# Zero fills of two gradient caches: nine fills on fifteen DMA engines become fills on sixteen, and four fills change place

## The chip, the core and the metric

The kernel runs on one core of a Trainium2 chip. A core has TensorE (matmuls, called PE in the profile), VectorE (DVE), ScalarE (ACT), GpSimd (POOL) and SyncE (SP), and sixteen DMA engines that carry all transfers between its on-chip memory and HBM. Transfers are issued by an engine's instruction stream, here mostly GpSimd's and SyncE's. The metric is the device time of one execution in microseconds (us), the median of several runs.

## What is computed

The reference is one decode step of a small transformer block with adaptive layer norm, its attention over a sliding window of a cache, a gated feed-forward part (FFN), and the gradients of all of it:

```python
mod = silu(c) @ w_mod                      # sa, ca, ga, sb, cb, gb
h = layernorm(x) * (1 + ca) + sa
x = x + ga * attention(h, k_cache, v_cache, wq, wo)   # the last 4096 of 65536 positions
h = layernorm(x) * (1 + cb) + sb
x = x + gb * ((sigmoid(h @ w_gate) * (h @ w_up)) @ w_down)
out, vjp = jax.vjp(f, x, k_cache, v_cache, wq, wo, w_gate, w_up, w_down, c, w_mod)
```

The outputs are `out` and a gradient for each input. What matters here are the gradients of the two caches (`out_2`, `out_3`): each is 4 heads x 65536 positions x 128 numbers in bf16, 64 MiB. Attention reads only the last 4096 positions, so the gradient of the first 61440 is zero. These zeros have to be written: 120 MiB, about half of all bytes that the kernel moves.

## The kernel before

**The zero fills.** The region of zeros of each head is seen as 128 rows of 61440 numbers and cut into 15 pieces of 128 rows x 4096 numbers, 1 MiB each; 2 caches x 4 heads x 15 pieces give 120 fills. A fill is one DMA from the small tile `zeros` on chip, issued by GpSimd. The list `zleft` holds them in order, and `zero(n, after)` (L147 to L171) issues the next `n`, if wanted not before a given instruction.

Of the 120 fills, 111 are wide (L169): 128 rows over all sixteen DMA engines, eight rows each. Nine are narrow (their places in the list are in `NARROW`). A narrow fill is two transfers. A piece of five rows of 512 bytes, in two halves (L162), takes the engines 0 to 4 after the cursor that deals out engines has been reset. It is followed by 120 of the 128 rows (L165), which take the next fifteen engines, so that the engine with index `SKIP` = 4 is left out. The eight rows left out of each narrow fill are written elsewhere: in the nine small pieces, and once near the start in `zero_rest` (two transfers, L361 and L364, of 540 KB and 13.5 KB).

**Where they are issued.** There is no scheduler: the order of instructions on each engine is the order of the program text. Counts written by hand say how many fills are issued at each point: `Z_Q` in the query projection, `Z_N` in the stage that forms a large product of keys and weighted values (`n_ps`, L636), `Z_B` in the chunks of the product with the output weights (`b_ps`, L691; called B), `Z_FOLD` at the end of the stage that folds the modulation weights, `Z_FFN` in the seven blocks of the FFN (four counts for each), `Z_END` in the last stage. GpSimd also issues most loads and stores in the same stream, so a fill stands in line with them.

**An FFN block.** The FFN's 3584 columns go through in seven blocks of 512. For block `q` the kernel forms the gradients of `w_up` and `w_gate` in place and stores them in two halves (`store_ug`, L868), with `zero(z[0])` and `zero(z[1])` behind these. It then starts block `q+1` with `front`, and handles its rows of `w_down` in two halves `s`: the forward matmul (`ffn_mm`, L970), a reduction (`wd_ttr`, L210), the gradient in place (`wd_outer`, L206) and its store (`store_wd`, L854). `zero(z[2])` follows the first half, `zero(z[3])` the second. The loads of block `q+2` are `load_ug` (L864, GpSimd) and `load_wd` (L851, SyncE); `load_wd` overwrites the buffer of the rows just stored, so it waits until that store has landed.

**The last stage** forms the remaining gradients (`wo`, `w_mod`, the window of the caches, `wq`) and stores them as they are ready; the kernel ends with stores of 512 KB to 1 MB, issued by GpSimd (L1125, L1130, L1166, L1173, L1177).

Of the kernel before, what the change touches and what calls it, by code (L numbers as in the profile page):

```python
# [10 lines left out]
P = 128  # L11
FP32 = mybir.dt.float32
# [21 lines left out]
EPS = 1e-5  # L34
SCALE = DH ** -0.5
KIB = 512
SKIP = 4
NARROW = (6, 18, 31, 44, 57, 70, 83, 96, 108)

def spread(total, n):
    return [(i + 1) * total // n - i * total // n for i in range(n)]
# [8 lines left out]
Z_KC = [0] * 8  # L51
Z_SM = 4
Z_N = spread(31, 128)
Z_B = [n + (i in (31, 38)) for i, n in enumerate(spread(29, 43))] + [1, 1, 1, 1, 0] + [1, 1, 0, 1, 1, 0, 1, 1] + [1, 0, 1, 0, 1, 0, 0, 0]
Z_FOLD = (1, 1, 3)
Z_FFN = [(1, 1, 0, 1)] * 5 + [(1, 1, 1, 2), (1, 2, 1, 0)]
Z_END = (1, 2, 1, 0, 0)
@with_exitstack
def kernel(
# [26 lines left out]
    nc = tc.nc  # L86
    SKW = A_k_cache.shape[2] - W
# [16 lines left out]
    def vt(shape, name, dt=FP32):  # L104
        return pool.tile(shape, dt, name=name)
# [4 lines left out]
    ZW = 4096  # L110
    zeros = vt([P, ZW // 2], "zeros", FP8)
# [11 lines left out]
    zregions = []  # L123
    for og in (out_2, out_3):
        for g in range(G):
            region = og[0, g, 0:SKW, :].rearrange("r d -> (r d)").rearrange("(p x) -> p x", p=P)
# [1 line left out]
                zregions.append(region[:, i * ZW:(i + 1) * ZW])  # L128

    narrow = zregions[0:len(NARROW)]
    wide = zregions[len(NARROW):]
    zleft = []
    while narrow or wide:
        if narrow and (len(zleft) in NARROW or not wide):
            zleft.append((narrow.pop(0), True))
        else:
            zleft.append((wide.pop(0), False))
    nlen = len(NARROW)
    ncount = list(range(1, nlen + 1))  # L140
    NS = SKIP + 1
    rest = out_2[0, 0, 0:SKW, :].rearrange("r d -> (r d)").rearrange("(p x) -> p x", p=P)[0:8, 0:nlen * ZW].bitcast(FP32)
    assert nlen * 2 <= 20

    keep = [0]

    def dep(later, earlier):  # L147
        tc.add_manual_dep(later.ins, earlier.ins.name,
                          mybir.DependencyInfo(mybir.DependencyClass.Sync, mybir.DependencyReason.DATA),
                          reason="pace")  # L150

    def zero(n, after=None):
        for _ in range(n):
            if len(zleft) <= keep[0]:
                return
            region, narrow_ = zleft.pop(0)
            first = None
            if narrow_:
                nc.gpsimd.inc_swdge_sem([], [], mode="reset_dge_cursor")  # L160
                n = nlen - ncount.pop()
                first = nc.gpsimd.dma_start(  # L162
                    out=rest[0:NS, 0:nlen * 128].rearrange("p (t x) -> p t x", t=2)[:, :, n * 64:(n + 1) * 64],
                    in_=zeros[0:NS, 0:64].rearrange("p (t x) -> p t x", t=1).broadcast_to([NS, 2, 64]))
                ins = nc.gpsimd.dma_start(  # L165
                    out=region[8:P, :].bitcast(FP32).rearrange("(t p) x -> p t x", t=2),
                    in_=zeros[0:60, :].rearrange("p (t x) -> p t x", t=1).broadcast_to([60, 2, ZW // 2]))
            else:
                ins = nc.gpsimd.dma_start(out=region.bitcast(FP32), in_=zeros[:, :])  # L169
            if after is not None:  # L170
                dep(first or ins, after)  # L171

    rot = [(psum, "mm")]
# [13 lines left out]
    def new_tp(name="tp"):  # L188
        p, tag = next_pool()
        return p.tile([P, 1024], BF16, name=name, tag=tag)  # L190
# [165 lines left out]
        nc.sync.dma_start(out=wq_t[j], in_=wq_view[:, j, :])  # L356
    load_kv(A_v_cache, v_nat)

    def zero_rest(after):
        wr = nlen * 120  # L360
        ins = nc.gpsimd.dma_start(out=rest[:, nlen * 128:].rearrange("p (t x) -> t p x", t=16),  # L361
                                  in_=zeros[0:16, 0:wr].rearrange("t (p x) -> t p x", p=1).broadcast_to([16, 8, wr]))
        dep(ins, after)
        nc.gpsimd.dma_start(out=rest[NS:8, 0:nlen * 128], in_=zeros[0:8 - NS, 0:nlen * 128])  # L364

    tp0 = new_tp("tp_rows")[:, 0:24]
    nc.tensor.transpose(tp0, rows24[:, :], ident_bf[0:24, 0:24])
    vecs = vt([P, 24], "vecs")
# [36 lines left out]
    for j in range(KD):  # L405
        for k in range(16):
            mm = nc.tensor.matmul(mod_ps[:, k:k + 1], lhsT=wm01_t[j][:, k * P:(k + 1) * P],
                                  rhs=cs_bf[:, j:j + 1], start=(j == 0 and k == 0), stop=(j == KD - 1),
                                  skip_group_check=True)
# [28 lines left out]
    jobs = []  # L438
# [24 lines left out]
    for j in range(KD):  # L463
        if j in (1, 2, 3):
            kT_unit(8 + 2 * j)
            kT_unit(9 + 2 * j)
        if 0 < j <= NT:
            for g in range(G):
                wqT_unit(j - 1, g, "AVAA"[g])
        for h in range(HQ):  # L470
            mm = nc.tensor.matmul(q_ps[:, h:h + 1], lhsT=wq_t[j][:, h * P:(h + 1) * P],  # L471
                                  rhs=h1_bf[:, j:j + 1], start=(j == 0 and h == 0), stop=(j == KD - 1),
                                  skip_group_check=True)
        zero(Z_Q[j], mm)
    zero_rest(mm)
    nc.scalar.activation(out=warm, in_=ones_f[:, 0:1], func=ACT.Exp)
    q_col2 = vt([P, 2 * HQ], "q_col2", BF16)
    cp(q_col2[:, 0:HQ], q_ps[:, 0:HQ])
# [4 lines left out]
    for ch in range(8):  # L483
        ps = new_ps("sc_ps")
        for g in range(G):
            mm = nc.tensor.matmul(ps[32 * g:32 * g + 32, 0:512], lhsT=q_col2[:, HG * g:HG * g + 32],
                                  rhs=k_T[:, g, ch * 512:(ch + 1) * 512], start=True, stop=True,
                                  tile_position=(0, 32 * g))
        nc.scalar.copy(out=P_bf[:, ch * 512:(ch + 1) * 512], in_=ps[:, :])
        nc.vector.reduce_max(out=mx8[:, ch:ch + 1], in_=ps[:, :], axis=AX.X)  # L490
        if ch % 2:
            wqT_unit(KD - 1, ch // 2, "AV"[ch // 2 % 2])
        zero(Z_KC[ch], mm)
# [115 lines left out]
    def mod_gb(ts_):  # L609
        ps = new_acc("g_ps")  # L610
        mod_tiles(ps, g_t, ts_, True, ts_[-1])
        if ts_[0] == 6:
            cp(gb, ps[:, 0:KD])
        else:
            addv(gb, gb, ps[:, 0:KD])
# [5 lines left out]
    def recent(mm, lag):  # L621
        last_mm.append(mm)
        return last_mm[-lag] if len(last_mm) >= lag else last_mm[0]

    for g in range(G):
        nbank = bank_pair("n_ps", g)
        for t_ in range(KT):
# [7 lines left out]
            for k in range(2):  # L635
                mm = nc.tensor.matmul(nbank[k][:, :], lhsT=k_nat[:, g, t_ * DH:(t_ + 1) * DH],  # L636
                                      rhs=vp[:, t_ % 2, 4 * k:4 * k + 4, :].rearrange("p h d -> p (h d)"),
                                      start=(t_ == 0), stop=False)
# [25 lines left out]
    bq = []  # L664
# [16 lines left out]
    def bch(n=1):  # L681
        for _ in range(n):
# [5 lines left out]
            for a in range(4):  # L688
                h = 4 * u + a
                for k in range(2):  # L690
                    mm = nc.tensor.matmul(bbank[p][k][:, :], lhsT=a4[:, p, h, :], rhs=wo_t[u][:, a, k * 512:(k + 1) * 512],  # L691
                                          start=(i == 0 and a == 0), stop=(i == 7 and a == 3))
            zero(Z_B[nbq - 1 - len(bq)], recent(mm, 3))
            if i == 7:
# [87 lines left out]
    def park(p, pl, tag):  # L782
        BT_ps[p] = pl.tile([P, D], BF16, name="BT_ps", tag=tag)
        for i in range(KD):
            nc.tensor.transpose(BT_ps[p][:, i * P:(i + 1) * P], B_t[p][:, i * P:(i + 1) * P], ident_bf[:, :])
# [64 lines left out]
    def load_wd(q, s):  # L850
        nc.sync.dma_start(out=wd_v[:, 2 * s:2 * s + 2, :], in_=wd_dram(B_w_down, q, s))  # L851
# [10 lines left out]
    def load_ug(q, j0, n):  # L862
        for k, view in ((0, wu_view), (1, wg_view)):
            nc.gpsimd.dma_start(out=ug_tile(q, k, j0, n), in_=ug_part(view, q, j0, n))  # L864
# [5 lines left out]
    def fold_half(t, k):  # L870
        ps = new_ps("fold_ps")
        for i in range(4):
            nb = 4 * k + i
            for x, src in enumerate((ga_t[t], cb_t[t], sb_t[t])):
                nc.tensor.matmul(ps[:, i * P:(i + 1) * P], lhsT=src[:, nb * P:(nb + 1) * P], rhs=ident_bf[:, :],  # L875
                                 start=(i == 0 and x == 0), stop=(x == 2), skip_group_check=True)
        nc.scalar.copy(out=w2_t[t][:, k * 512:(k + 1) * 512], in_=ps[:, :])  # L877
# [45 lines left out]
    fold_half(7, 1)  # L923
    zero(Z_FOLD[0])
    park(4, ppq, "pq")
    load_ug(1, 0, 4)
    load_ug(1, 4, 4)
    zero(Z_FOLD[1])
    mod_gb((0, 1, 2, 3, 4, 5))
# [48 lines left out]
    def wd_outer(q, s):  # L978
        for i in (2 * s, 2 * s + 1):
            outer_dve(wd_v[:, i, :], small[q % 2]["hh"][:, i:i + 1], b1k)  # L980
        store_wd(q, s)
# [30 lines left out]
    wd_outer(0, 1)  # L1012
    zero(Z_FOLD[2])
    load_wd(1, 0)
    load_wd(1, 1)
    for q in range(NB):
        z = Z_FFN[q]
        more = q + 1 < NB
# [282 lines left out]
    s2(7)  # L1301
    keep[0] = 0
    zero(len(zleft))
    assert not zleft and not narrow and not jobs and not bq

# [1 line left out]
_INS = ['A_x', 'A_k_cache', 'A_v_cache', 'A_wq', 'A_wo', 'B_x', 'B_w_gate', 'B_w_up', 'B_w_down', 'c', 'w_mod', 'grad_out']  # L1307
# [26 lines left out]
```

## Time and profile before

The time is 600.43 us (median of 3 runs, 600.42 to 600.61). The profiled execution has a span of 600.9 us.

| What | Value |
|---|---|
| bytes moved by DMA | 246.64 MB, mean 410 GB/s |
| read from HBM, written to HBM | 60.30 MB, 185.60 MB |
| transfers in GpSimd's queue (q0) | 216.55 MB |
| transfers in SyncE's and ScalarE's queue (q1) | 29.37 MB |
| wide fills, 1024 KB each | 111, 14.6 us from issue to landing (median) |
| narrow fills, 960 KB each | 9, 14.1 us |
| small pieces of the narrow fills, 2.5 KB each | 9, 12.4 us |
| `zero_rest`, 540 KB and 13.5 KB | 10.8 us and 10.5 us |
| a fill's instruction on GpSimd | 0.53 us wide, 0.60 and 0.67 us for the two of a narrow one |

A page of the profile gives for each engine its busy time and share, then the span in 40 slices of 15 us with a digit for the busy tenths of each, the DMA row and the rate of the transfers. The views of waits name the engine and line that waited, after "<-" what ended the wait, then total us, how many times, and the longest. The chain of waits is followed back from the last instruction; each piece of it is listed with its start, its length and what it was spent on.

### The profile page before, as it was taken

The numbers are of one execution on the slowest core, as the hardware profiler recorded it, in microseconds if no ns is written. First come the engines' busy times: TensorE is split into PE (matmuls) and PEld (weight loads), VectorE is DVE, ScalarE is ACT, GpSimd is POOL, SyncE is SP. The second block draws the span as 40 slices with busy tenths as digits, with TensorE's granted clock in tenths as the row PEclk, the third lists the DMA queues.
The fourth block names the chain that finished last, engine by engine and source line by source line (L and its number), as shares of the span: only waits on it lengthen the run. The fifth ranks groups of instructions, "written<-read, shape, count | busy, mean of one in ns | idle before, by whom it ended". The sixth has DMA issues, their size and how long they took to land.

```text
span 600.9 us, 11073 instructions
## 1 busy us (share of the span) xinstructions
PE 411.7 (69%) x4612; PEld 276.5 (46%) x4612; DVE 327.1 (54%) x620; ACT 284.7 (47%) x429; POOL 164.2 (27%) x265
## 2 busy tenths in 40 slices
PE   3997689999999989999985245444444196856300
PEld 3995334334344546546554234434434175655300
DVE  3654499999511010160008286695686888768430
ACT  3489514567212014212226556965857866863200
POOL 0003123223222222222322324333343253222230
PEclk9999699999999999999985555555555586755555
DMA  8999999999999999999999999999999999999995
GB/s 349 420 417 422 413 424 412 427 423 424 426 423 425 423 427 422 423 424 425 420 404 406 418 374 401 398 409 415 406 413 415 418 406 414 419 425 427 422 417 240
DMA packets 45171, 246.64 MB, mean 410 GB/s; under 512 B 5253, under 2 KB 5253, under 8 KB 24712
## 3 DMA queue, kind: packets, MB, share of 16 engines
q0 software_dynamic: 38976, 216.55, 94.4%
q1 hardware_dynamic: 6096, 29.37, 12.6%
q8 instruction: 36, 0.59, 0.4%
q14 instruction: 15, 0.12, 0.1%
q10 hardware_dynamic: 48, 0.01, 0.0%
HBM read 60.30 MB, written 185.60 MB: 409 GB/s over the span
## 4 chain that ended last, share of the span: by engine, by line
PE 40%; DMA 28%; DVE 17%; ACT 8%; issue 4%; POOL 0%; ACTq 0%; POOLq 0%; SPq 0%; DVEq 0%
DMA out_dram<-arena 19%; PE b_ps L691 17%; PE n_ps L636 6%; DMA arena<-in_B_w_down_dram 6%; DVE junk L210 4%; DVE arena L193 4%; DVE arena L206 4%; ACT arena L241 3%; DMA arena<-in_B_w_gate_dram 3%; PE t_ps L598 2%; DVE arena L210 2%; PE w_ps L394 2%; PE tp_wq L453 2%; PE fold_ps L875 1%; PE tp_k L434 1%
## 5 line engine op out<-in xcount | busy, mean ns | idle before, releaser
L691 PE MATMUL b_ps<-arena 128*128 128x512 bf16 x512 | 116.2, 379 | 0.0
L169 POOL DMA_DIRECT2D out_dram<-zeros x111 | 60.4, 545 | 197.3 <-PE q_ps L471 50.9
L836 PE MATMUL tp_side<-ident_bf,arena 128*128 128x128 bf16 x432 | 52.5, 303 | 45.9 <-ACT arena L837 39.0
L837 ACT COPY arena<-tp_side 128x1024 bf16<-128x1024 bf16 x54 | 53.9, 1012 | 52.5 <-PE tp_side L836 52.0
L193 DVE TENSOR_TENSOR arena<-arena 128x2048 bf16<-128x2048 bf16 x64 | 76.5, 1223 | 2.3 <-PE n_ps L636 0.3
L691 PEld LDWEIGHTS <-arena 128*128 128x128 bf16 x512 | 48.8, 98 | 55.8 <-issue 2.9
L210 DVE CUSTOM_DVE_ANT_0 arena<-arena,scr 128x1024 bf16<-128x1024 bf16 x56 | 65.2, 1220 | 10.3 <-ACT scr L990 10.3
L636 PE MATMUL n_ps<-arena 128*128 128x512 bf16 x256 | 65.7, 378 | 6.2 <-DVE arena L193 4.6
L836 PEld LDWEIGHTS <-arena 128*128 128x128 bf16 x432 | 43.6, 140 | 50.4 <-issue 50.1
L241 ACT ACTIVATE arena<-scr,h 128x1024 bf16<-128x1024 bf16 x56 | 61.5, 1146 | 1.4 <-DVE dh2acc L210 1.3
L636 PEld LDWEIGHTS <-arena 128*128 128x128 bf16 x256 | 24.6, 97 | 41.6 <-issue 16.2
L210 DVE CUSTOM_DVE_ANT_0 junk<-arena,b1k 128x1024 bf16<-128x1024 bf16 x28 | 34.2, 1222 | 11.6 <-DMA arena<-in_B_w_down_dram 11.1
L1161 ACT ACTIVATE arena<-ps_kv 128x512 bf16<-128x512 f32 x48 | 26.2, 686 | 28.8 <-PE ps_kv L1157 28.5
L868 POOL DMA_DIRECT2D out_dram<-arena x28 | 21.0, 755 | 64.8 <-ACT arena L241 40.3
L202 DVE CAST arena<-b_ps 128x512 bf16<-128x512 f32 x6 | 4.1, 691 | 61.6 <-PE b_ps L691 61.6
L600 ACT CAST arena<-t_ps 128x512 bf16<-128x512 f32 x56 | 30.1, 589 | 12.1 <-PE t_ps L598 12.1
L1157 PE MATMUL ps_kv<-junk,arena 8*128 8x128 bf16 x256 | 27.3, 305 | 11.7 <-DVE arena L206 10.6
L1157 PEld LDWEIGHTS <-arena 8*128 8x128 bf16 x256 | 25.3, 141 | 13.5 <-issue 13.5
L455 ACT COPY arena<-tp_wq 128x1024 bf16<-128x1024 bf16 x23 | 21.7, 1044 | 8.2 <-PE tp_wq L453 8.2
L970 PE MATMUL fg<-hh_bf,arena 128*128 128x1 bf16 x224 | 8.2, 166 | 22.7 <-DMA arena<-in_B_w_down_dram 20.9
L877 ACT CAST arena<-fold_ps 128x512 bf16<-128x512 f32 x16 | 9.4, 586 | 24.1 <-PE fold_ps L875 24.1
L206 DVE TENSOR_SCALAR arena<-arena,cs_col 128x4096 bf16<-128x4096 bf16 (+1 forms) x16 | 16.0, 1018 | 8.3 <-DMA out_dram<-arena 8.2
(299 smaller groups left out, 644.4 us busy)
## 6 DMA issues: line engine op xcount, KB each, us to landing
out_dram<-zeros POOLq DMA_DIRECT2D x111, 1024.0 KB, 14.6
out_dram<-arena POOLq DMA_DIRECT2D x32, 1024.0 KB, 18.2
out_dram<-arena POOLq DMA_DIRECT2D x50, 512.0 KB, 9.6
out_dram<-zeros POOLq DMA_DIRECT2D x9, 960.0 KB, 14.1
arena<-in_A_wq_dram SPq DMA_DIRECT2D x8, 1024.0 KB, 20.5
arena<-in_A_wo_dram POOLq DMA_DIRECT2D x8, 1024.0 KB, 12.2
arena<-in_w_mod_dram POOLq DMA_DIRECT2D x7, 1024.0 KB, 18.6
arena<-in_B_w_down_dram SPq DMA_DIRECT2D x14, 512.0 KB, 8.2
```

The costliest lines, as they stand in the source:

```text
L169: ins = nc.gpsimd.dma_start(out=region.bitcast(FP32), in_=zeros[:, :])
L193: return nc.vector.tensor_tensor(out=out, in0=a, in1=b, op=op)
L206: return nc.vector.tensor_scalar(out=out, in0=a, scalar1=s1, scalar2=None, op0=op0)
L210: return nc.vector.tensor_tensor_reduce(out=out, in0=w, in1=b, scale=1.0, scalar=0.0, op0=ALU.mult, op1=ALU.add, accum_out=acc)
L241: return nc.scalar.activation(out=out, in_=b, func=ACT.Copy, scale=col)
L600: nc.scalar.copy(out=o, in_=ps)
L636: mm = nc.tensor.matmul(nbank[k][:, :], lhsT=k_nat[:, g, t_ * DH:(t_ + 1) * DH], rhs=vp[:, t_ % 2, 4 * k:4 * k + 4, :].rearrange("p h d -> ...
L691: mm = nc.tensor.matmul(bbank[p][k][:, :], lhsT=a4[:, p, h, :], rhs=wo_t[u][:, a, k * 512:(k + 1) * 512], start=(i == 0 and a == 0), stop= ...
L836: nc.tensor.transpose(tp[:, i * P:(i + 1) * P], blk[:, i * P:(i + 1) * P], ident_bf[:, :])
L837: nc.scalar.copy(out=blk if dst is None else dst, in_=tp[:, :])
L1157: nc.tensor.matmul(ps[:, t4 * DH:(t4 + 1) * DH], lhsT=rows[32 * g:32 * g + HG, t_ * P:(t_ + 1) * P], rhs=hd[32 * g:32 * g + HG, :], start= ...
L1161: nc.scalar.activation(out=o, in_=ps[:, :], func=ACT.Copy, scale=float(scale))
```

## The change

All 120 fills become wide: nothing is skipped, `zero_rest` and the small pieces are gone, and the list of fills is simply the list of regions. With it four fills change place. One chunk of B loses its fill (`Z_B`), the two at the end of the fold stage go (`Z_FOLD`), and the last FFN block loses one (`z[2]` of the last entry). They return in the FFN: one more in the blocks 0, 1 and 2 between the two halves of `w_down`, and one more in block 5. The change makes all fills alike and spreads them more evenly over the FFN.

```diff
-SKIP = 4
-NARROW = (6, 18, 31, 44, 57, 70, 83, 96, 108)
...
-Z_B = [n + (i in (31, 38)) for i, n in enumerate(spread(29, 43))] + [1, 1, 1, 1, 0] + [1, 1, 0, 1, 1, 0, 1, 1] + [1, 0, 1, 0, 1, 0, 0, 0]
-Z_FOLD = (1, 1, 3)
-Z_FFN = [(1, 1, 0, 1)] * 5 + [(1, 1, 1, 2), (1, 2, 1, 0)]
+Z_B = [n + (i in (31, 38)) for i, n in enumerate(spread(29, 43))] + [1, 1, 1, 1, 0] + [1, 1, 0, 1, 1, 0, 1, 1] + [1, 0, 0, 0, 1, 0, 0, 0]
+Z_FOLD = (0, 0, 3)
+Z_FFN = [(1, 1, 1, 1)] * 3 + [(1, 1, 0, 1)] * 2 + [(1, 1, 1, 3), (1, 2, 0, 0)]
...
-            region, narrow_ = zleft.pop(0)
-            first = None
-            if narrow_:
-                nc.gpsimd.inc_swdge_sem([], [], mode="reset_dge_cursor")
-                n = nlen - ncount.pop()
-                first = nc.gpsimd.dma_start(
-                    out=rest[0:NS, 0:nlen * 128].rearrange("p (t x) -> p t x", t=2)[:, :, n * 64:(n + 1) * 64],
-                    in_=zeros[0:NS, 0:64].rearrange("p (t x) -> p t x", t=1).broadcast_to([NS, 2, 64]))
-                ins = nc.gpsimd.dma_start(
-                    out=region[8:P, :].bitcast(FP32).rearrange("(t p) x -> p t x", t=2),
-                    in_=zeros[0:60, :].rearrange("p (t x) -> p t x", t=1).broadcast_to([60, 2, ZW // 2]))
-            else:
-                ins = nc.gpsimd.dma_start(out=region.bitcast(FP32), in_=zeros[:, :])
+            ins = nc.gpsimd.dma_start(out=zleft.pop(0).bitcast(FP32), in_=zeros[:, :])
...
-    zero_rest(mm)
```

## The prediction

> **What bounds the kernel.** I start with the slices and the share of each engine.
>
> ```profile
> PE 411.7 (69%) x4612; PEld 276.5 (46%) x4612; DVE 327.1 (54%) x620; ACT 284.7 (47%) x429; POOL 164.2 (27%) x265
> ...
> DMA  8999999999999999999999999999999999999995
> GB/s 349 420 417 422 413 424 412 427 423 424 426 423 425 423 427 422 423 424 425 420 404 406 418 374 401 398 409 415 406 413 415 418 406 414 419 425 427 422 417 240
> ```
>
> No compute engine is over 69% of the span, while the DMA row shows 9 from the second slice to the last but one. The rate is 412 to 427 GB/s up to slice 19 and 374 to 418 in slices 21 to 34, mostly the FFN blocks. The program is a transfer program: 246.64 MB, of which 120 MiB are the zero fills. A change in fills matters through the sixteen DMA engines, not through an instruction.
>
> Next, who waits for transfers: GpSimd's waits over the whole span, TensorE's in the FFN (310 to 486 us), and SyncE's.
>
> ```profile
> POOL out_dram L169 <- DMA out_dram<-zeros: 43.3, 24, 3.2
> ...
> PE fg L970 <- DMA arena<-in_B_w_down_dram: 20.9, 10, 7.8
> ...
> SPq L851 <- DMA out_dram<-arena: 140.1, 12, 30.5
> ```
>
> GpSimd waits 24 times for an earlier fill to land. The reason is in the completion semaphores: its transfers take eight of them in turn, so a fill is issued only when the transfer eight before it has landed on all sixteen engines. Example: the fill issued at 259.24 follows the landing, at 258.71, of the one issued at 240.18. So the last of the sixteen engines sets the pace of issue. The w_down lines close a loop in the FFN: a load waits for the store of the same buffer, and TensorE and VectorE wait for the load.
>
> Last, the chain of waits from 484 us:
>
> ```profile
> 508.42 21.89 DMA out_dram<-arena
> ...
> 545.95 19.75 DMA out_dram<-arena
> ...
> 568.74 14.47 DMA out_dram<-arena
> ```
>
> The end is a full store queue. What the last engine still has to move then is end time, one for one.
>
> **Reading single DMA engines.** The trace holds sixteen completion times for each transfer, without engine numbers. I sort the sixteen of each GpSimd transfer and compare each with the ninth ("the middle"). A 1 MiB fill lands 2.44 us after the one before it (middle of 110), so an engine's 64 KB share costs 2.44 us.
>
> Narrow fills stand out. At the one issued at 138.10 (L165) one engine goes from 1.56 ahead of the middle (L162's piece, 148.38) to 3.92 ahead (the next wide fill, 153.15). That engine is the one skipped. The other eight show the same step: **2.33 us each**.
>
> Between narrow fills this engine falls back, smoothly: 3.92 to 3.06 ahead (153 to 185 us), 5.35 to 4.18 (190 to 222), 6.57 to 5.64 (227 to 257), 8.70 to 7.23 (268 to 297). The others keep their places but for single jumps. It loses 0.86 us in 32, 1.17 in 32, 0.93 in 30, 1.47 in 29: about 3% to 5%, taken as **3.1%**. So the skipped engine is a slow one. In the busy stage it is still over-relieved: 7 us ahead at 297 us, 8.9 ahead of the second earliest at 305.
>
> **What the Trainium skill says.** "DMA: Bandwidth & Descriptors", section "Why a DMA increments its semaphore by 16 and not by 1": on GpSimd's path all sixteen engines post a completion whatever the shape, and a transfer over fewer engines takes consecutive ones from a cursor. The trace agrees: even a five-row piece has sixteen completions, and one engine lands about 0.2 us after its last work while the others need 2.25. Same page, "Latency and other measured facts": engines 7 and 15 are usually slower in traces. The trace has no engine numbers and the kernel skips index 4, so only "one is slower" is confirmed, at 3.1%. Same page, "Anatomy of one DMA": about 2.0 us fixed plus bytes over 436e3. For 512 KB that is an estimate of 3.2 us; the store issued into a nearly empty queue at 480.86 took 3.37 to the middle landing. A latency above that is queue.
>
> **The change, part by part.**
>
> 1. Pieces that disappear. L361 costs 64.97 - 63.58 = 1.39 us of every engine, L364 0.19, nine L162 0.2 each = 1.8. Sum **3.4 us less** for all engines. Bytes are the same: 111 + 9 whole fills.
>
> 2. GpSimd's instructions. Eleven fewer, at 0.53 to 0.60 us (lines L361, L364, L162), and nine of 0.67 become 0.53: 7.6 us. GpSimd is 27% busy and waits for landings; hidden behind those waits, priced at nothing.
>
> 3. The slow engine's share. It now takes part in nine more fills: 9 x 2.33 = **21.0 us more** work.
>
> 4. The credit it wasted before. An engine far ahead runs dry, since GpSimd holds back for the last engine. From 305 to 356 us the skipped engine goes from 8.9 us ahead of the second earliest to level; 1.7 of these are its own slowness, some 1.7 more fall to reordering with SyncE's loads, leaving 5.5. Smaller losses of the same kind: 1.4 at 92 us, 0.7 at 376, 1.0 at 475 to 484, 0.8 in scattered places. Sum **9.4 us** idle before that work can fill.
>
> 5. Idle time shared by all. The middle engine shows some 3 us of gaps from 300 to 490 us (1.05 at 357, others of 0.1 to 0.8). The slow engine, now last with a backlog, need not have them: **0 to 3 us**, I take 3.
>
> 6. The moved fills: one chunk fill of B, both fold fills and one of the last block go to blocks 0 to 2 (after the first w_down store) and block 5. It is 4 x 2.44 = 9.8 us of transfers moved, none added. All of them stand behind the gate/up loads of block 0 (issued 289.23 to 296.48), so these gain nothing; the chunk fill (299.89) and the first fold fill (307.45) stand ahead of block 1's loads, which come 4.9 us sooner in the queue. Behind the inserted GpSimd instruction are the second w_down store and the loads of the block after next; SyncE's load waits for that store. The cost is bounded by 0 (the queue is full anyway, and the fill only takes the place of another one) and 3 x 2.44 = 7.3 (each block prolonged, nothing returned). I take 0.
>
> Sum at the end. Before, the last store lands at 597.99 on its last engine, 597.62 on the one before. I take the skipped engine for the last one, because the last place drifts from 2.55 to 3.40 behind the middle between 525 and 555 us as no other does. After: 597.99 + 21.0 - 3.4 - 9.4 - 3 = 603.2, so **+5.2 us**. If it was not last but in the middle (594.4), the sum gives 1.6; if the gaps in 5 stay, 8.2.
>
> A second way, by the FFN's start. The gate load that starts it lands in the middle at 311.61, last at 312.97. After: 311.61 + 7.1 (3.1% of 228 us) - 3.0 (pieces up to there) = 315.7, 2.7 later than before. From there the middle took 282.8 us to 594.4, with as many fills after as before; less 3 gaps, plus 3.1% of 282 = 8.7: 288.5. End 604.2, +6.2. The two ways share the drift but not the credit, and they agree within 1 us.
>
> Prediction: 600.43 + 5.2 = **605.6 us**.
>
> **The rivals.**
>
> A, chance 0.14, faster: the drift belongs to the profiled execution alone, and the timed runs have no slow engine. Then narrow fills only cost their pieces: 600.43 - 3.4 = 597.0. For it: nothing in an untimed profile can exclude it. Against: the span with the profile, 600.9, is within 0.1% of the timed 600.43, and fifteen engines with the same records to write show no such drift.
>
> B, chance 0.11: the slow engine was in the middle of the pack at the end and takes its extra work out of idle time. 1.6 less part of the uncertain credit: 600 to 602, say 601. About half of this is within 0.2%.
>
> C, chance 0.09: the inserted fills prolong the w_down loop by more than they return, because the load and the store in it are each paced by the slow engine: half of the 7.3 on top, 609.3. For it: L970's 20.9 us of waits. Against: TensorE's waits there show the loop stretched by backlog already, and the total is fixed by bytes.
>
> D, the forecast, chance 0.66: 602 to 608.
>
> **Numbers.** Slower: D 0.66, C 0.09, and 0.05 of B = 0.80. Same 0.06. Faster 0.14. The range runs from 600.6, which leaves out A and the low end of B, to 609.0, which keeps the upper bound of step 5 and leaves out about half of C.
>
> **What would show it.** After: the issue table has one row of 120 fills of 1024 KB. In the sixteen completions of the fills one engine drifts steadily behind, 6 to 7 us behind the middle near 300 us, where one was 7 ahead. GpSimd's waits for landed fills grow above 43.3 us, since it waits for that engine. GB/s in slices 21 to 39 falls by about 2%. The last store's sixteen completions spread by 6 us or more instead of 4.9. Step 6 is wrong if blocks 0 to 2 are longer than before by more than 2.4 us each and later blocks are not shorter. The prediction is wrong if no engine drifts, or if the drifting engine finds idle time to catch up.

## The result, and the profile after

The changed kernel takes **609.84 us** (median of 6 runs, 609.29 to 612.06) against 600.52 (600.42 to 600.68) for the kernel before: a ratio of 1.0159, 95% interval 1.0144 to 1.0175. The change costs 9.3 us. The prediction, 605.6, had the direction and the cause; its size was 4.2 us short, and 609.84 lies 0.84 outside its range.

The page of the profile after (span 607.6 us): the engines' busy time, the DMA row and the rate in 40 slices of 15.2 us, and the row of the fills among the DMA issues (count, KB each, median us from issue to landing).

```profile
PE 413.0 (68%) x4612; PEld 277.9 (46%) x4612; DVE 326.9 (54%) x620; ACT 285.8 (47%) x429; POOL 156.4 (26%) x254
...
DMA  9999999999999999999996999999999999999993
GB/s 350 420 417 422 412 429 417 426 425 426 423 425 424 426 427 421 426 423 426 413 381 263 413 406 414 409 412 416 408 408 418 422 419 417 419 424 423 420 414 152
...
out_dram<-zeros POOLq DMA_DIRECT2D x120, 1024.0 KB, 15.4
```

The compute engines are busy as long as before (TensorE 413.0 against 411.7 us), and all 120 fills are wide. The rate isn't lower everywhere. It has one hole, 381 and 263 GB/s where before had 404 and 406, and the last slice has fallen from 240 to 152: one engine finishes after the others, as the completions below show.

GpSimd's waits over the whole span (us in all, times, longest):

```profile
POOL out_dram L143 <- DMA out_dram<-zeros: 59.5, 33, 4.3
```

Before it was 43.3 us in 24 waits. The sixteen completion times of single transfers say why. Sorted, in us from the ninth ("the middle"), for transfers at like places:

```
before, middle 155.58   -3.80 -0.86 ...  0.00 ...  1.37  1.44
after,  middle 156.66   -1.57 -1.50 ...  0.00 ...  1.57  2.24
before, middle 226.94   -6.57 -0.92 ...  0.00 ...  1.61  2.24
after,  middle 225.59   -1.70 -1.66 ...  0.00 ...  1.47  4.43
before, middle 277.36   -8.26 -2.17 ...  0.00 ...  0.95  1.44
after,  middle 276.06   -3.04 -3.00 ...  0.00 ...  1.38  5.31
after,  middle 295.69   -3.05 -3.00 ...  0.00 ...  1.44  7.70
last store, before, middle 594.36   -1.24 -1.23 ...  0.00 ...  3.27  3.64
last store, after,  middle 598.20   -1.53 -1.52 ...  0.00 ...  0.94  6.67
```

The kernel before had one engine alone at the left end. In the changed kernel one engine stands alone at the right end and drifts away from the other fifteen. The last store is complete at 598.20 + 6.67 = 604.87, where before ended at 597.99 or so; its middle engine is only 3.8 us later.

**The hole.** Engine windows of 310 to 335 us, after and then before. The columns are the window, its length, busy us and count of PE, PEld, DVE, ACT and POOL, then the granted clock, the DMA share and GB/s.

```profile
310.00:335.00 25.00, 12.88 (x216) 11.30 (x217) 15.33 (x34) 11.16 (x14) 4.97 (x8) 0.56 0.82 307
```

```profile
310.00:335.00 25.00, 12.33 (x197) 10.83 (x195) 17.05 (x36) 14.41 (x17) 7.75 (x13) 0.55 1.10 411
```

The chain of waits after, where the FFN starts and at the end:

```profile
297.38 18.91 DMA arena<-in_B_w_gate_dram
316.33 1.75 PE fg L919 x59
...
552.85 19.75 DMA out_dram<-arena
...
575.65 14.49 DMA out_dram<-arena
```

The FFN starts when the first block's gate load has landed on the last engine: 316.3, before 312.97. GpSimd's list of instructions (start, us, line, transfer, in brackets how long it was idle before and for what), after and then before:

```profile
314.12 0.75 POOL L830 DMA_DIRECT2D arena<-in_B_w_gate_dram  x1 [0.87 <-DMA arena<-in_B_w_gate_dram]
...
322.59 0.56 POOL L820 DMA_DIRECT2D out_dram<-arena  x1 [7.73 <-DVE arena L180]
...
326.61 1.59 POOL L143 DMA_DIRECT2D out_dram<-zeros  x3
```

```profile
315.71 0.56 POOL L169 DMA_DIRECT2D out_dram<-zeros  x1 [1.45 <-DMA out_dram<-zeros]
319.27 0.56 POOL L854 DMA_DIRECT2D out_dram<-arena  x1 [3.00 <-DVE arena L206]
```

For 7.73 us GpSimd has nothing to issue: it waits for the first `w_down` gradient, which waits for the FFN's start, which waits for the slow engine. The fills that stood here before have been moved to behind that gradient. So fifteen engines run dry. The slow one still has its backlog and hardly stops: its completions follow one another at 327.03, 328.29, 329.60 and 332.22 us, for transfers of 512, 512, 512 and 1024 KB. Its lag behind the middle falls from 6.4 to 0.6 us, and it grows again to 6.7 by the end. The hole is time that the fifteen lose, not the engine that ends last.

TensorE's waits for FFN loads, 310 to 490 us. Before, they were 20.9 us for `w_down` and, for the gate load:

```profile
PE fg L953 <- DMA arena<-in_B_w_gate_dram: 3.2, 4, 1.2
```

After:

```profile
PE fg L919 <- DMA arena<-in_B_w_gate_dram: 9.8, 6, 2.3
PE fg L936 <- DMA arena<-in_B_w_down_dram: 5.9, 4, 1.7
PE fg L919 <- DMA arena<-in_B_w_up_dram: 5.7, 3, 2.8
```

The `w_down` wait went to the gate and up loads, 21.4 us in all against 24.1: the moved fills relieve one load and delay another. (In the experiments below, the kernel with the moves alone waits 5.3 us for `w_down` and 14.5 for gate and up, the one with the wide fills alone 22.2 and 2.9.) From the first block's first activation to the last block's the FFN takes 143.96 us, where it took 143.61.

### The profile page after: what moved, and what is told of

It reads as the page before. It is cut to its first block, busy times and chain, and to the rows that moved or that the text cites. A ratio compares the mean times of both kernels' runs of the same rounds, so it can differ in the third digit from the quotient of the medians.

```text
span 607.6 us, 11049 instructions
## 1 busy us (share of the span) xinstructions
PE 413.0 (68%) x4612; PEld 277.9 (46%) x4612; DVE 326.9 (54%) x620; ACT 285.8 (47%) x429; POOL 156.4 (26%) x254
## 3 DMA queue, kind: packets, MB, share of 16 engines
q1 hardware_dynamic: 6096, 29.37, 12.7%
## 4 chain that ended last, share of the span: by engine, by line
PE 38%; DMA 32%; DVE 14%; ACT 7%; issue 5%; POOL 1%; ACTq 0%; POOLq 0%; SPq 0%; DVEq 0%
DMA out_dram<-arena 18%; PE b_ps L657 14%; DMA arena<-in_B_w_gate_dram 7%; PE n_ps L602 6%; DVE arena L167 4%; DVE junk L184 4%; DMA arena<-in_w_mod_dram 3%; ACT arena L215 3%; DMA arena<-in_B_w_down_dram 3%; DVE arena L180 3%; PE tp_wq L420 2%; PE t_ps L564 2%; DVE arena L184 2%; PE w_ps L361 2%; PE tp_side L802 1%
## 5 line engine op out<-in xcount | busy, mean ns | idle before, releaser
L143 POOL DMA_DIRECT2D out_dram<-zeros x120 | 66.3, 554 | 209.5 <-DMA out_dram<-zeros 59.5
L657 PE MATMUL b_ps<-arena 128*128 128x512 bf16 x512 | 117.8, 383 | 0.0
L657 PEld LDWEIGHTS <-arena 128*128 128x128 bf16 x512 | 49.2, 99 | 56.7 <-issue 4.5
L184 DVE CUSTOM_DVE_ANT_0 arena<-arena,scr 128x1024 bf16<-128x1024 bf16 x56 | 65.2, 1220 | 10.3 <-ACT scr L956 10.3
L802 PEld LDWEIGHTS <-arena 128*128 128x128 bf16 x432 | 44.2, 140 | 54.9 <-issue 54.6
L602 PEld LDWEIGHTS <-arena 128*128 128x128 bf16 x256 | 24.6, 97 | 41.6 <-issue 16.2
L919 PE MATMUL fg<-h_bf,arena 128*128 128x1 bf16 x448 | 14.8, 166 | 15.6 <-DMA arena<-in_B_w_gate_dram 9.8
L919 PEld LDWEIGHTS <-arena 128*128 128x128 bf16 x448 | 14.1, 106 | 16.4 <-DMA arena<-in_B_w_gate_dram 10.3
## 6 DMA issues: line engine op xcount, KB each, us to landing
out_dram<-arena POOLq DMA_DIRECT2D x50, 512.0 KB, 10.3
```

The source lines that it names most:

```text
L143: ins = nc.gpsimd.dma_start(out=zleft.pop(0).bitcast(FP32), in_=zeros[:, :])
L184: return nc.vector.tensor_tensor_reduce(out=out, in0=w, in1=b, scale=1.0, scalar=0.0, op0=ALU.mult, op1=ALU.add, accum_out=acc)
L802: nc.tensor.transpose(tp[:, i * P:(i + 1) * P], blk[:, i * P:(i + 1) * P], ident_bf[:, :])
L919: nc.tensor.matmul(gu[:, col + i:col + i + 1], lhsT=ug_v[:, q % 2, j // 4, j % 4, k, f0:f0 + 255:2], rhs=h2_bf[:, j:j + 1], start=(j == 0) ...
```

## Experiments

**The two halves of the change.** One kernel moves the four fills and keeps the narrow ones, the other makes all fills wide and leaves every place as it was.

```diff
 # before, with the places of after
-Z_FOLD = (1, 1, 3)
+Z_FOLD = (0, 0, 3)
 # and Z_B, Z_FFN as in the change
```

> The kernel before with only the four fills moved (the nine narrow fills stay). Theory S (one DMA engine, the skipped one, is some 3% slow and its total work sets the end): its work is unchanged, so 600 to 602 us. Theory M (the 9.3 us come from the moved fills: after, the queue ran empty at the start of the FFN, 307 GB/s between 310 and 335 us): most of the loss shows here, 605 to 610 us.

Measured: 601.86 us against 600.71, ratio 1.0029 (1.0016 to 1.0042), as theory S has it. The window of the hole:

```profile
310.00:335.00 25.00, 11.90 (x190) 10.52 (x187) 16.98 (x35) 14.31 (x17) 5.65 (x10) 0.53 1.00 370
```

```diff
 # after, with the places of before
-Z_FOLD = (0, 0, 3)
+Z_FOLD = (1, 1, 3)
 # and Z_B, Z_FFN as in before
```

> All 120 fills wide, but every fill where it was before. Theory S: the slow engine has its nine shares more, 607 to 611 us, and one of the sixteen completions lags 6 to 7 us at the end. Theory M: 597 to 602 us, since only small pieces went away.

Measured: 610.69 us, ratio 1.0163 (1.0148 to 1.0179), again as theory S has it; the last store's last completion is 6.2 us behind the middle. The fills' waits on GpSimd, the rate by slices and the window one FFN block later, for the all-wide kernel:

```profile
POOL out_dram L143 <- DMA out_dram<-zeros: 57.9, 32, 4.3
```

```profile
GB/s 351 419 416 423 412 426 419 426 424 428 422 425 424 426 427 421 426 425 425 413 410 403 398 294 397 410 409 405 399 407 407 411 393 419 420 421 428 423 416 168
```

```profile
335.00:360.00 25.00, 8.91 (x148) 7.79 (x148) 11.62 (x27) 11.38 (x14) 8.80 (x13) 0.50 0.98 337
```

The wide fills alone bring the whole loss. The places decide only where the hole lies: at 381 and 263 GB/s with the moved fills, at 398 and 294 two slices later without. With the narrow fills kept, the moves cost 0.29% by themselves (window 310 to 335: 370 GB/s against 411); together with the wide fills they add nothing that these intervals resolve.

**Which engine is skipped.** The nine fills stay narrow and leave out index 6 in place of index 4.

```diff
-SKIP = 4
+SKIP = 6
```

> The kernel before, but the narrow fills leave out the engine with index 6 instead of 4. Theory S: the slow engine gets no relief and still the small pieces, 610 to 614 us; one engine runs ahead without falling back and another drifts behind. Theory L (it is not one slow engine, but fewer packets in nine fills or the engine that runs ahead that help): 599 to 602 us.

Measured: 610.69 us, ratio 1.0164 (1.0147 to 1.0180), as bad as no narrow fill at all. One engine runs up to 10 us ahead. Between narrow fills its lead doesn't wear off smoothly: it is 5.98 us at 156 us and 6.01 at 185, where that of index 4 went from 3.80 to 3.08. (Near 235 and 281 us it loses 3.4 and 4.4 us at once.) Meanwhile another engine drifts to 6.9 us behind (321 us). Relief helps only on the engine that is slow, and that one is index 4, counted from the reset cursor; no trace shows the engines' own numbers.

**How much relief is used.** Five, two, five with the last one later, and six narrow fills, all else as before.

```diff
-NARROW = (6, 18, 31, 44, 57, 70, 83, 96, 108)
+NARROW = (18, 44, 70, 96, 108)      # five
+NARROW = (44, 96)                   # two
+NARROW = (18, 44, 70, 96, 118)      # five, the last later
+NARROW = (18, 40, 62, 84, 106, 118) # six
```

> The kernel before with five narrow fills (places 18, 44, 70, 96, 108) instead of nine. Theory S: 4 x 2.33 = 9.3 us less relief, of which some was wasted before: 602 to 606 us. If relief was wasted to a larger part than 9.4 us: 600 to 601. If there is no slow engine: about 599, four small pieces less.

Measured: 600.35 us, ratio 0.9990 (0.9975 to 1.0004), below the 602 to 606 that theory S gave and inside its second case: five do what nine did. The four further shares of work for the slow engine cost nothing, so about that much relief, some 9 us, had been wasted.

> The kernel before with two narrow fills (places 44 and 96). Theory S, with the measured 600.4 us for five and 610.7 for none: each share that the slow engine moves more costs 2.33 us less some 0.4 for a piece, so 605 to 607 us, on a straight line. If a few fills matter for another reason (a break in the order of the queues), 600 to 603.

Measured: 605.22 us, ratio 1.0083 (1.0066 to 1.0099), inside the expected 605 to 607; the last store is complete at 596.01 + 4.31. None, two, five and nine give 610.7, 605.2, 600.35 and 600.7. The first two bring 5.5 us, where the expectation's straight line had 2 x (2.33 - 0.4) = 3.9; with intervals of some 1 us on either side of each time, that is barely more. The next three bring 4.9, the last four nothing.

> The kernel before with five narrow fills, the last of them moved to place 118, in the last stage, where TensorE issues most instructions per us. Theory S: with five at 18 to 108 the slow engine ended last, 1.2 us behind the next; one share at the right time takes that away: 598.5 to 600 us. If the end is set by other engines or by the order of the stores: 600.2 to 600.8.

Measured: 599.42 us, ratio 0.9977 (0.9968 to 0.9987).

> The kernel before with six narrow fills, the last at place 118. Theory S: as with five and the last one late, 598.5 to 600 us, or 0.2 more for the piece if the slow engine is no longer the last. If relief is worth most early: 600 to 601.

Measured: 599.48 us, ratio 0.9982 (0.9975 to 0.9988). Both lie in the expected 598.5 to 600 us and are faster than the kernel before by 0.2%, and by 1.7% than the change. Their last narrow fill goes out near the end of the fills, so the slow engine is nearly level with the rest at the last store: for six, it is complete at 592.72 + 1.54, for five with the last one late at 593.17 + 2.06. Whether the late place itself helps isn't settled: the intervals of the two kernels with five overlap (0.9975 to 1.0004 and 0.9968 to 0.9987). GpSimd's waits and the slices, six:

```profile
POOL out_dram L169 <- DMA out_dram<-zeros: 34.6, 19, 3.5
```

```profile
GB/s 350 420 418 420 413 426 413 427 420 428 427 418 424 424 429 422 424 423 424 424 396 410 422 408 416 410 410 407 407 412 415 414 411 412 421 424 424 425 418 283
```

No hole is left, and the last slice moves 283 GB/s instead of 152. (With five at the first places, the waits are 53.1 us and the time is that of before, so the waits themselves aren't the cost.)

**What makes the engine slow.** Five kernels leave the whole computation out but for the 120 fills, and put one stream of instructions beside them. Their times are of one execution each, so the readings rest on the completions.

```diff
+    zero(len(zleft))                      # the fills alone
+    for i in range(3000):                 # second: 128 columns; third: range(780), 512 columns
+        nc.tensor.matmul(pe_ps[i % 2][:, 0:128], lhsT=ident_bf[:, :], rhs=pe_w[:, 0:128], start=True, stop=True)
+    for i in range(3000):                 # fourth: no matmuls, this instead
+        nc.vector.tensor_copy(out=dv[1], in_=dv[0])
```

> Only the 120 wide fills, one after the other, eight in flight; all of the computation and the other outputs are left out, TensorE, VectorE and ScalarE have nothing to do. Theory P (the slow engine loses time to something that goes with TensorE's instructions: in the kernel after it fell back by 3 to 4% where TensorE issued 6 matmuls per us, by about 8% at 14 per us, and hardly at the end): no engine drifts, the sixteen completions of the last fill spread by under 3 us, 120 fills take about 293 us. Theory C (that engine is always slow): one engine drifts by 3%, some 9 us at the end.

Measured: 300.83 us; the sixteen completions of the last fill lie within 0.45 us. No engine is slow by itself.

> The same 120 fills, and beside them 3000 matmuls of 128 columns on constant data (10 or more per us); the computation is left out. Theory P: one engine drifts behind by 5 to 8% for as long as the matmuls last. Theory C: 3%, as without them.

Measured: 314.92 us. One engine lags 2.5 us behind the earliest at 52 us and 14.2 at 275. That window:

```profile
52.00:275.00 223.00, 156.45 (x2254) 154.39 (x2252) 0.00 (x0) 46.22 (x87) 0.84 1.15 426
```

It lost 11.7 us in 223, or 5.2%, beside 4506 TensorE instructions (matmuls and weight loads): **2.6 ns for each**. The same holds fill by fill, since the matmuls come in bursts: the 12 fills beside which TensorE issued nothing took this engine 2.46 us on average, the 26 beside which it issued 90 or more took 2.68.

> The same 120 fills beside 780 matmuls of 512 columns: TensorE is about as busy, with a quarter of the instructions; the computation is left out. If it is the number of instructions, the drift is a quarter of that beside 3000 matmuls, 1 to 2%; if it is TensorE's busy time or its reading of on-chip memory, it is the same or more.

Measured: 304.38 us. TensorE runs to about 176 us and is busier while it does, with fewer instructions:

```profile
52.00:163.00 111.00, 111.00 (x517) 50.30 (x515) 0.00 (x0) 23.48 (x45) 1.00 1.15 427
163.00:300.00 137.00, 9.22 (x43) 3.98 (x41) 0.00 (x0) 26.04 (x49) 0.55 1.13 420
```

The lag behind the earliest engine grows from 1.37 to 3.72 us in the first window, 2.3 ns for each of 1032 instructions, and from 3.86 at 180 us, when TensorE has stopped, to 3.95 at 298. With TensorE busy 100% of the time and half the instructions per us, the engine loses 2.1% instead of 5.2%: the loss goes with the **number of instructions**, not with TensorE's busy time, nor with the columns it reads (517 x 512 in 111 us against 2254 x 128 in 223). Each matmul here has a weight load, so which of the two costs the time isn't separated.

> The same 120 fills beside 3000 small copies on VectorE; the computation is left out. If instructions of any engine slow that DMA engine: a drift like that beside as many matmuls. If only TensorE's do: none, and perhaps another engine drifts.

Measured: 659.91 us, set by the copies, which outlast the fills; the time tells nothing. In the completions two engines, not one, lag at 273 us, 4.64 and 6.75 behind the middle, in two ways. The first falls back smoothly from 0.78 at 52 us: 1.7%, 3.9 ns for each of 1002 VectorE instructions. The second goes from 1.41 to 6.75 in eight steps of 0.8 to 1.0 us, one every 27 us or so, and doesn't fall back between them; each step comes with an 8 KB packet of an instruction queue (at 79.1, 107.3, 135.5 us and so on). The window, and that queue over the whole span (packets, MB):

```profile
52.00:273.00 221.00, 186.33 (x1002) 46.76 (x88) 1.00 1.15 427
...
q14 instruction: 24, 0.20, 0.1%
```

Which index the first one has, no run tells.

Fifth, the 3000 matmuls with five narrow fills that leave out index 4:

```diff
+SKIP = 4
+NARROW = (15, 36, 57, 78, 99)
```

> The 120 fills beside 3000 matmuls of 128 columns, five of the fills narrow, without the engine of index 4; the computation is left out. If the engine that TensorE's instructions slow is the one with index 4: the lag of the last engine, 11.6 us without narrow fills, falls to 1 to 3 us and the time from 314.9 to 303 to 307 us. If it is another engine: the lag stays and one engine runs ahead, 314 to 317 us.

Measured: 317.17 us, a miss of the expected 303 to 307, because the matmuls lasted longer than the fills: 217 of the 3000 ran after 300 us. The chain of waits by line:

```profile
by line: PE pe_ps L186 67.8%; issue 31.4%; DVEq L212 0.2%; DVE pe_w L183 0.1%; DVE ones_f L121 0.0%
```

The fills themselves answer the question: the last one lands at 301.05 in the middle and 1.62 later on the last engine, where without narrow fills it was 10.5 (11.9 at most, at 280 us). The engine that TensorE's instructions slow is index 4.

## Why the prediction was right, and where it fell short

**Reading which engine is slow: right.** The prediction took the engine that fell back between narrow fills as a slow one at 3.1%. After the change it drifts at 3.8% between 157 and 276 us (3.81 to 8.35 behind the earliest engine); beside 1020 TensorE instructions between 157 and 238 us it loses 2.87 us, 2.8 ns for each, so the rate of the small kernels accounts for it. It isn't a constant, as the prediction used it: 8.4% from 490 to 528 us, where TensorE runs 28 instructions per us (1.2 us of these 3.25 come in one step at 522 us), and hardly any from 548 us on (131 matmuls in 52 us). The Trainium skill, "DMA: Bandwidth & Descriptors", section "Latency and other measured facts", names engines 7 and 15 as usually slower; here it is the one at index 4 under TensorE's instructions, and no engine under fills alone.

**Step 3 failed in its size: a share costs the slow engine 2.54 us, not 2.33.** The 2.33 is what this engine gains on the middle when it is left out. Its own share costs more: the prediction's 2.44 us and 3.1% would have given 2.52. In the trace after, from the fill that lands at 156.66 to the one at 237.82, it takes 84.0 us for 33 transfers of 1 MiB; in the trace before, 32.9 us for 13 (153.15 to 185.18), 2.53 each. Nine shares are then 22.9 us, 1.9 more than the 21.0 of step 3. The sum ended at 603.2 in the profiled execution; the last store is complete at 604.87, 1.7 later. With 22.9, the other steps left as they were, it ends at 605.1; since steps 4 and 5 are estimates, that fit isn't a proof of each. Nor do all nine narrow fills show a step of 2.33, as the prediction reads them: four do (2.29 to 2.39, from 138 to 265 us), the first two show 1.8 and 1.6, and at the last three it is mixed with other movements.

**Carrying the difference over failed too, and is the larger part of the miss.** The difference was worked out inside the profiled execution of before, which took 602.65 us, and added to the median of the timed ones, 600.43. The prediction held its span, 600.9, against that median and found them alike; but a span is not a time: the profiled execution of after has a span of 607.6 and took 609.39. From profile to profile the change costs 6.7, near the 7.1 of the sum with step 3 put right; from median to median it costs 9.3. The miss of 4.2 is 1.7 (the sum), 2.2 (602.65 - 600.43) and 0.4 (609.84 - 609.39), less 0.1 because the profile after ends sooner behind its last store. Where the profiled execution of before lost its 2.2 us stays open.

**Steps 1, 2 and 4: nothing on record speaks against them.** With 2.54 for a share, five fills should bring 5 x 2.54 = 12.7, less 1.0 for five pieces and 0.9 for a `zero_rest` that shrinks with their number: 10.8 us. The runs give 610.69 - 600.35 = 10.3, with intervals of about 1 us on each time. Step 4, 9.4 us of wasted credit, stands against the four narrow fills that the five-fill kernel does without: 4 x 2.54 = 10.2 us more work for the slow engine, 1.5 less for pieces, and 0.4 us less time, so some 9 were wasted. Step 2: GpSimd's busy time fell 7.8 us and the time did not.

**Step 5 stays open.** It let the slow engine use up 3 us of idle time that all engines share. No run isolates it. The prediction had gaps closing and none opening, and the hole is a gap that opened; but it hardly touches the slow engine. It does end that engine's backlog, so from 329 us on it can be short of work like the others.

**The second way came nearer, partly by luck.** It put the FFN's start at 315.7 (measured 316.3) and gave 288.5 us from there; 604.87 - 316.3 is 288.6. But it holds a constant 3.1% and the 3 us of step 5, the one known to be wrong and the other not measured, so errors in it may cancel. That the two ways agreed within 1 us proved little, since both share these terms.

**Step 6: right for this change.** Blocks 0 and 1 take 22.7 and 23.4 us (before 22.7 and 29.6), blocks 2 and 3 take 25.8 and 26.0 (22.2 and 21.9). Block 2 is longer by more than 2.4 us, but blocks 0 to 2 together are 2.6 us shorter, and the six blocks together as long as before. But the moves aren't free where the narrow fills stay: 0.29%, where the prediction had 0.

**What would show it.** One row of 120 fills: yes. Drift to 6 to 7 us behind near 300 us: 6.15 at 293, then two steps of 1.5 us to 9.1 at 298. GpSimd's waits above 43.3: 59.5. The last store's spread of 6 us or more: 1.53 + 6.67 = 8.2. A fall of the rate by about 2% in slices 21 to 39: the mean falls from 410.9 to 405.6, 1.3%, but all of it in slices 21 and 22; from slice 23 on it is 0.9% higher.

**The rivals.** A, drift in the profiled execution only and faster timed runs, is out: the timed runs lose 9.3 us, the profile 6.7. B, 600 to 602 us, is out. C's number, 609.3, is near, but its cause is not it: with every fill in its old place the loss is 1.63%, with the moved ones 1.59%.

**Open.** Why a TensorE instruction costs that engine 2.6 ns. The Trainium skill, "Runtime: NRT & Kernel Launch", section "Instruction fetch mechanics", says that a sequencer fetches instructions in blocks of 16 KB over a DMA queue of its own, mostly hidden. The trace of before agrees on the size in one instruction queue:

```profile
q8 instruction: 36, 0.59, 0.4%
```

Beside the 3000 matmuls of 128 columns, single engines in turn fall back by 1.2 to 1.4 us at once, some 14 us apart, as these packets are. Those are steps on changing engines, so they aren't the steady drift. Whether the recording of instructions plays a part, no run here tells: the timed runs lose no less than the profiled ones, but each of them, too, is listed with a span and a granted clock, so none is known to be free of records.

## What to carry to other kernels

When transfers bound a kernel, sort the sixteen completion times of its transfers before touching any: an engine at one end that moves steadily showed here what no row of the page did, and its speed can be read from the slope. Give a slow engine as little relief as keeps it level with the rest up to the end: five or six narrow fills, the last one late, did slightly better than nine. Price a share of work at what it costs the engine that has to do it. Work out a difference against the execution whose time it is added to, or take the median's own profile.

## What the runs showed of the hardware

Fills alone load all sixteen engines alike (last fill complete within 0.45 us, 120 fills in 300.83 us). Beside a stream of TensorE instructions one DMA engine, index 4, is slower by 2.3 to 2.6 ns for each matmul or weight load: 5.2% at 20 of them per us, 2.1% at 9 per us with TensorE always busy, 0.1 us in 118 when it has stopped. Beside VectorE copies one engine is slower by about 3.9 ns for each, and another loses 0.8 to 1.0 us at a time, together with 8 KB packets of an instruction queue. A transfer that waits for all sixteen engines is paced by the slowest, and leaving index 4 out of 5 of 120 fills is worth 10.3 us of 610.7.
